# Attention's result in feature rows: division by sums broadcast over partitions, in place of two rounds of transposes

## The chip, the cores and the metric

One core of a Trainium2 chip. The metric is device time in microseconds of the whole kernel; the kernel before takes 807.38 us, the median of three runs (806.86 to 809.02). TensorE (PE in the profile) does the matmuls and the transposes, its weight loads are shown as PEld; VectorE is DVE, ScalarE is ACT, GpSimd is POOL, and SP issues DMAs.

## The reference

Attention over 2 x 8 heads of 768 positions with 64 features, in which a query sees only the keys of its own bucket (6 random hyperplanes hash both), and then two MLPs over 1536 tokens, 512 to 2048 to 512.

```python
mask = q_bucket[:, :, :, None] == k_bucket[:, :, None, :]
scores = np.where(mask, scale * np.matmul(q, k.transpose(0, 1, 3, 2)), -1000000000.0)
attn = np.exp(scores - np.max(scores, axis=-1, keepdims=True))
attn = attn / (np.sum(attn, axis=-1, keepdims=True) + 1e-09)
x = np.matmul(attn, v).transpose(0, 2, 1, 3).reshape(B * S, H * D)
x = softplus(x @ w_in) @ w_out                       # softplus: max(h, 0) + log1p(exp(-abs(h)))
h = x @ w2_in
return (h * np.clip(h + 3.0, 0.0, 6.0) / 6.0) @ w2_out
```

## The kernel before

The kernel writes no order of work by hand. Each step is added to a plan (`plan.add`) with the engines that may do it and a cost for each (A is ScalarE, D VectorE, P GpSimd, T TensorE, S an issue on SP), what it reads and writes, and a priority: the head's number times `TH` plus a constant of the table `WHEN`. For a DMA the plan also has a transfer time (`dma=`), and it lets a DMA go only when the eighth before it has landed. `Schedule.run` goes through modelled time, takes on each engine the ready step of lowest priority number, and emits it; the order of emission is the order on each engine's queue, and waits follow from buffers. Buffers with a tag and a number rotate: a new one waits until the last user of the old one is done.

Attention (`attend`, lines 413 to 529) runs per head over six tiles of 128 queries. Per tile: two halves of scores (lines 430 and 431, each a product of high parts and one of the rest and of the bucket bits), the negated row maximum on VectorE (444), a small step for bias and scale (451), exp on ScalarE (459) which also sums each row into `den`, six transposes of the result (470), and a copy out of PSUM into `et` (`even`, by the helper on lines 242 and 244). Scores and transposes share three PSUM buffers, `two0` to `two2`. When a head's six tiles are done, the values' product (486) runs in three steps. It gives `av`, 128 partitions by 384: partition u x 64 + d is feature d, column i x 128 + q is query q of tile 3u + i. So it comes with features in partitions, but two halves of the queries one above the other.

Behind it the kernel before goes to query rows and back. ScalarE copies `av` to `xa` (line 502), TensorE transposes its three blocks into PSUM (`pt`, line 508), GpSimd adds 1e-9 to the sums (512), VectorE takes the reciprocal (516) and multiplies, a reciprocal per partition and tile, into `xn` (523), queries in partitions, with 64 columns for each of two heads. When both heads of a pair are in, `to_features` (541 to 560) transposes the six tiles again (line 550, in groups of four and two) into `xt`, features of both heads in 128 partitions, and takes from PSUM the high part `xh` (ScalarE, line 242) and the rest `xl` (VectorE, line 247), the first MLP's input.

One PSUM bank each has the tags `pre` and `av`; the hash products `d` (372), `av`, `pt` and `xt` take whichever comes free, and later the first MLP's `ph`.

Beside attention the plan puts the loads of later heads and the weights of four of the MLPs' eight column blocks, each of which VectorE and ScalarE convert from two words to float pairs (lines 592 to 625). SP issues nearly all loads of the heads and the SBUF copies of query parts (359) and of bucket bits (403). The first MLP begins once the last scores are issued, between the last head's steps. The remaining weights are loaded when all buffers of the pool `tail` are done (`close_attention`).

Of the kernel before, what the change touches and what calls it, by code (L numbers as in the profile page):

```python
# [20 lines left out]
P = 128  # L21
# [10 lines left out]
BITS = 3  # L32
EX = 3

TH = 10.540
# [18 lines left out]
def f32(ap):  # L54
    return ap.bitcast(F32)
# [130 lines left out]
def lsh_attention_two_mlps(  # L186
# [33 lines left out]
    def open_pool(name, where, **kw):  # L220
        pools[name] = where.enter_context(tc.tile_pool(name=name, bufs=1, **kw))

    attention, heads = ctx.enter_context(ExitStack()), ctx.enter_context(ExitStack())
    for name in ("x", "w", "bits"):
        open_pool(name, ctx)
    open_pool("ps", ctx, space=PSUM)
    open_pool("tail", attention, side="right")
    open_pool("heads", heads)
# [11 lines left out]
    def cast(e, out, in_):  # L240
        if e == "A":
            nc.scalar.activation(out, in_, AF.Copy)  # L242
        else:
            engines[e].tensor_copy(out, in_)

    def minus(e, out, a, b):
        engines[e].tensor_tensor(out, a, b, op=ALU.subtract)
# [165 lines left out]
    def attend(h):  # L413
        at = h * TH
        if h % 2 == 0:
            xn[h // 2] = buffer("tail", [P, NT, P], F32, "xn", 2, f"xn{h // 2}")

# [74 lines left out]
        for c in range(0, NT, 2):  # L492
# [5 lines left out]
            ]  # L498
        xa = buffer("tail", [P, HALF], F32, "xa", 2, f"xa{h}")
        plan.add(  # L500
            dict(A=0.44), lambda e: cast(e, xa.ap, av.ap[:, :HALF]),
            reads=[av], writes=[xa], prio=at + WHEN["back"],
        )
        pt = buffer("ps", [P, 512], F32, ("pre", "av"), 1, f"pt{h}")

        def back(e):
            for i in range(n):
                nc.tensor.transpose(pt.ap[:, i * P : (i + 1) * P], xa.ap[:, i * P : (i + 1) * P], ident.ap)  # L508

        plan.add(dict(T=0.25), back, mode="t", reads=[xa, ident], writes=[pt], prio=at + WHEN["back"])  # L510
        plan.add(
# [6 lines left out]
        )  # L518
        x = xn[h // 2]

        def norm(e):
            place = x.ap.rearrange("p (u i) d -> p i u d", u=2)[:, :, :, (h % 2) * D : (h % 2 + 1) * D]
            nc.vector.tensor_tensor(
                place, pt.ap[:, :HALF].rearrange("p (i u d) -> p i u d", u=2, d=D),
                rec.ap.rearrange("p (u i) -> p i u", u=2).unsqueeze(3).to_broadcast([P, n, 2, D]), op=ALU.mult,
            )

        plan.add(dict(D=0.5), norm, reads=[pt, rec], writes=[x], prio=at + WHEN["norm"])
        return last_scores, exp

# [10 lines left out]
    def to_features(hp_all, first, n):  # L541
        b, hp = divmod(hp_all, H // 2)
        g, off = divmod(b * NT + first, 4)
        at = (2 * hp_all + 1) * TH
        pt = buffer("ps", [P, 512], F32, ("pre", "av"), 1, f"xt{hp_all}_{first}")
        place = lambda x: x[0, g].ap[:, hp, off * P : (off + n) * P]

        def turn(e):
            for i in range(n):
                nc.tensor.transpose(pt.ap[:, i * P : (i + 1) * P], xn[hp_all].ap[:, first + i, :], ident.ap)  # L550

        plan.add(dict(T=0.085 * n), turn, mode="t", reads=[xn[hp_all], ident], writes=[pt], prio=at + WHEN["x"])
        hi = plan.add(
            dict(A=0.053 + 0.107 * n), lambda e: cast(e, place(xh), pt.ap[:, : n * P]),
            reads=[pt], writes=[xh[0, g]], prio=at + WHEN["x_high"],
        )
        plan.add(
            dict(D=0.069 + 0.133 * n), lambda e: minus(e, place(xl), pt.ap[:, : n * P], f32(place(xh))),
            reads=[pt], writes=[xl[0, g]], prio=at + WHEN["x_low"], after=[hi],
        )  # L560
# [305 lines left out]
```

## Time and profile before

| | |
|---|---|
| median of three runs | 807.38 us |
| the profiled execution, its span | 806.4 us (1.0 us less than that median) |
| PE busy, matmuls and transposes | 780.0 us, 97% |
| PEld, weight loads | 598.0 us, 74% |
| VectorE busy | 533.9 us, 66% |
| ScalarE busy | 484.6 us, 60% |
| DMA moved | 58.6 MB, mean 73 GB/s |
| granted TensorE clock | full in all 40 slices |

The page gives the share of the whole span. Attention is the first third (to some 260 us), the MLPs the rest, and VectorE and ScalarE are far busier in the first than in the second. PE is busy in both, but its durations contain the way through the array and overlap, so what a matmul costs is read from the distance of two starts.

### The profile page before, as it was taken

Reading aid. Unit: us, or ns where it says so; the run is one execution under the profiler, and the core shown is the slowest. Engines: PE = TensorE matmul, PEld = TensorE weight load, DVE = VectorE, ACT = ScalarE, POOL = GpSimd, SP = SyncE. Lnnn points to the kernel's source line nnn. Section 1 sums busy time; section 2 is a strip of 40 time slices with the busy share of each in tenths; the row PEclk is TensorE's granted clock in tenths of the full one; section 3 lists DMA queues with packets and bytes.
Section 4 is the critical chain, followed back from the end, with each engine's and each line's share of the span. In section 5 each row is a group of like instructions: output and inputs, shape, how many; then the busy total and the mean of one; then the engine's idle time right before and its main releaser. Section 6 shows DMA issues by size and latency. Waiting matters only on the chain.

```text
span 806.4 us, 10352 instructions
## 1 busy us (share of the span) xinstructions
PE 780.0 (97%) x3808; PEld 598.0 (74%) x3808; DVE 533.9 (66%) x942; ACT 484.6 (60%) x817; POOL 9.4 (1%) x53
## 2 busy tenths in 40 slices
PE   6799999999999999999999999999999999999997
PEld 3466666666667777888888888878888888888886
DVE  6699899886765899965454799989952322232222
ACT  4688998888875877766555777766542322231222
POOL 1000000000000000000000000000000000000000
PEclk9999999999999999999999999999999999999999
DMA  6645445432310470000000355540000100010001
GB/s 176 163 138 143 125 149 149 124 111 73 89 30 15 154 260 2 0 1 1 0 1 1 104 207 185 183 156 1 1 0 1 53 0 1 1 52 1 1 0 53
DMA packets 26354, 58.61 MB, mean 73 GB/s; under 512 B 3584, under 2 KB 7552, under 8 KB 26304
## 3 DMA queue, kind: packets, MB, share of 16 engines
q1 hardware_dynamic: 22896, 49.56, 19.9%
q10 hardware_dynamic: 3408, 8.39, 3.2%
q8 instruction: 30, 0.49, 0.3%
q14 instruction: 20, 0.16, 0.1%
HBM read 48.89 MB, written 3.15 MB: 65 GB/s over the span
## 4 chain that ended last, share of the span: by engine, by line
PE 87%; ACT 7%; DVE 2%; DMA 2%; issue 1%; SPq 0%; ACTq 0%; DVEq 0%
PE ph L645 33%; PE acc L738 17%; PE acc L740 16%; PE av L486 7%; PE tp L470 6%; PE sc L430 4%; PE sc L431 3%; ACT e L459 3%; ACT et L242 2%; DMA raw<-in_moe_w_in_dram 1%; ACT qa L330 1%; DVE nm L444 1%; ACT ka L242 1%; PE pt L508 1%; PE xt L550 0%
## 5 line engine op out<-in xcount | busy, mean ns | idle before, releaser
L645 PE MATMUL ph<-xh,w 128*128 128x512 f32 x768 | 240.2, 394 | 0.0
L645 PEld LDWEIGHTS ph<-xh,w 128*128 128x128 f32 x768 | 143.9, 188 | 32.6
L645 PE MATMUL ph<-xl,w 128*128 128x512 f32 x384 | 151.1, 393 | 0.0
L674 DVE SCALAR_TENSOR_TENSOR ml<-me,ph 128x512 f32<-128x512 f32 x48 | 33.0, 688 | 117.8 <-ACT me L669 117.5
L669 ACT ACTIVATE me<-ph,three 128x512 f32<-128x512 f32 x48 | 33.1, 689 | 125.7 <-PE ph L645 122.8
L459 ACT ACTIVATE e<-sc,bs 128x768 f32<-128x768 f32 x96 | 94.8, 990 | 22.2 <-DVE bs L451 21.5
L444 DVE TENSOR_REDUCE nm<-sc 128x1 f32<-128x768 f32 x96 | 89.5, 951 | 25.6 <-PE sc L431 25.1
L738 PE MATMUL acc<-gh,w 128*128 128x512 f32 x384 | 98.9, 395 | 0.0
L740 PE MATMUL acc<-w,gh 128*128 128x512 f32 x384 | 98.0, 393 | 0.0
L470 PEld LDWEIGHTS tp<-ident,e 128*128 128x128 f32 x576 | 63.7, 142 | 37.1 <-ACT e L459 22.4
L470 PE MATMUL tp<-ident,e 128*128 128x128 f32 x576 | 80.0, 280 | 7.3 <-ACT e L459 6.2
L738 PEld LDWEIGHTS acc<-gh,w 128*128 128x128 f32 x384 | 71.3, 188 | 18.6 <-ACT gh L242 2.1
L645 PEld LDWEIGHTS ph<-xl,w 128*128 128x128 f32 x384 | 72.1, 188 | 16.8
L740 PEld LDWEIGHTS acc<-w,gh 128*128 128x128 f32 x384 | 72.1, 188 | 16.8
L430 PE MATMUL sc<-ka,qa 128*128 128x384 f32 x192 | 73.2, 381 | 6.4 <-ACT et L242 5.8
L486 PE MATMUL av<-et,vx 128*64 128x384 f32 x384 | 71.4, 497 | 0.0
L242 ACT ACTIVATE et<-tp 128x768 f32<-128x768 f32 x78 | 62.5, 811 | 12.6 <-PE tp L470 11.8
L431 PE MATMUL sc<-kb,qb 96*128 96x384 f32 x192 | 66.5, 346 | 0.4 <-DVE kb L384 0.4
L705 DVE SCALAR_TENSOR_TENSOR me<-mu,me 128x512 f32<-128x512 f32 x48 | 33.1, 690 | 36.6 <-ACT mu L700 36.6
L738 PE MATMUL acc<-gl,w 128*128 128x512 f32 x192 | 53.6, 393 | 0.7 <-ACT xh L242 0.7
L740 PE MATMUL acc<-w,gl 128*128 128x512 f32 x192 | 53.5, 393 | 0.0
L242 ACT ACTIVATE w<-bits 128x512 fp32r<-128x512 f32 x64 | 39.9, 628 | 21.1 <-DVE bits L616 21.1
(65 smaller groups left out, 948.2 us busy)
## 6 DMA issues: line engine op xcount, KB each, us to landing
raw<-in_moe_w_in_dram SPq DMA_DIRECT2D x24, 512.0 KB, 4.4
raw<-in_moe_w_out_dram SPq DMA_DIRECT2D x24, 512.0 KB, 3.5
rawk<-in_kv_dram SPq DMA_DIRECT2D x15, 384.0 KB, 3.6
raw<-in_moe_w_in_dram ACTq DMA_DIRECT2D x8, 512.0 KB, 4.1
raw<-in_moe_w_out_dram ACTq DMA_DIRECT2D x8, 512.0 KB, 3.8
raw<-in_kv_dram SPq DMA_DIRECT2D x16, 192.0 KB, 3.6
raw<-in_q_dram SPq DMA_DIRECT2D x16, 192.0 KB, 4.0
vx<-in_kv_dram SPq DMA_DIRECT2D x16, 192.0 KB, 2.5
```

Source lines behind the costliest of these rows:

```text
L242: nc.scalar.activation(out, in_, AF.Copy)
L430: nc.tensor.matmul(o, qa[h].ap[:, qs], ka[h].ap[:, cs], start=True, stop=False)
L431: nc.tensor.matmul(o, qb[h].ap[0:KB, qs], kb[h].ap[0:KB, cs], start=False, stop=True)
L444: lambda e, sc=sc, t=t: nc.vector.reduce_max(nm.ap[:, t, 0:1], sc.ap[:, :, :HALF], axis=AX.XY, negate=True),
L459: lambda e, sc=sc, ex=ex, t=t: nc.scalar.activation(ex.ap.rearrange("p (u k) -> p u k", u=2), sc.ap[:, :, :HALF], AF.Exp, bias=bs.ap[:, t, ...
L470: nc.tensor.transpose(o, ex.ap[:, c * P : (c + 1) * P], ident.ap)
L486: nc.tensor.matmul(av.ap[u * D : (u + 1) * D, :HALF], vx[h].ap[:, c, :], et[u].ap[:, c, :], start=(c == 0), stop=(c == NT - 1),)
L645: nc.tensor.matmul(bank(), w[:, a, :], x[b].ap[:, kc, :], start=(kc + i == 0), stop=(kc == KC - 1 and i == 2))
L669: dict(A=0.478), lambda e: nc.scalar.activation(e1.ap, bank(), AF.Relu, bias=three.ap),
L705: lambda e: nc.vector.scalar_tensor_tensor(e1.ap, u.ap, -1.0, e1.ap, op0=ALU.add, op1=ALU.subtract),
L738: nc.tensor.matmul(o, w.ap[:, a, cs], b.ap, start=st, stop=sp)
L740: nc.tensor.matmul(o, b.ap[:, cs], w.ap[:, a, :], start=st, stop=sp)
```

## The change

The result of the values' product stays with features in partitions. The reciprocals, which lie with queries in partitions, are written to DRAM (`row`), and from there read back twice with the partition broadcast over 64 partitions each into `wide`, whose columns are queries, with the three tiles side by side at every query (a step of three in the multiplication). VectorE multiplies `av` in PSUM by `wide` into `xa`. Two DMAs per head copy the halves of `xa` to `xn`, now 128 partitions of features by 768 queries, side by side. `to_features` takes `xh` and `xl` from `xn` in SBUF. The ScalarE copy of `av`, the three transposes `pt` per head and the six transposes `xt` per pair go. All five new DMAs are on SP; `wide` and `xa` have one buffer each. The constants in `WHEN` stay.

```diff
-            xn[h // 2] = buffer("tail", [P, NT, P], F32, "xn", 2, f"xn{h // 2}")
+            xn[h // 2] = buffer("tail", [P, S], F32, "xn", 2, f"xn{h // 2}")
...
-        xa = buffer("tail", [P, HALF], F32, "xa", 2, f"xa{h}")
-        plan.add(
-            dict(A=0.44), lambda e: cast(e, xa.ap, av.ap[:, :HALF]),
-            reads=[av], writes=[xa], prio=at + WHEN["back"],
-        )
-        pt = buffer("ps", [P, 512], F32, ("pre", "av"), 1, f"pt{h}")
-
-        def back(e):
-            for i in range(n):
-                nc.tensor.transpose(pt.ap[:, i * P : (i + 1) * P], xa.ap[:, i * P : (i + 1) * P], ident.ap)
-
-        plan.add(dict(T=0.25), back, mode="t", reads=[xa, ident], writes=[pt], prio=at + WHEN["back"])
...
-        def norm(e):
-            place = x.ap.rearrange("p (u i) d -> p i u d", u=2)[:, :, :, (h % 2) * D : (h % 2 + 1) * D]
-            nc.vector.tensor_tensor(
-                place, pt.ap[:, :HALF].rearrange("p (i u d) -> p i u d", u=2, d=D),
-                rec.ap.rearrange("p (u i) -> p i u", u=2).unsqueeze(3).to_broadcast([P, n, 2, D]), op=ALU.mult,
-            )
-
-        plan.add(dict(D=0.5), norm, reads=[pt, rec], writes=[x], prio=at + WHEN["norm"])
+        row = buffer("rows", [2, P, n], F32, "row", 2, f"row{h}")
+        wide = buffer("tail", [P, P, n], F32, "wide", WIDE, f"wide{h}")
+        xa = buffer("tail", [P, n, P], F32, "xa", 1, f"xa{h}")
+        plan.add(
+            dict(S=0.625),
+            lambda e: engines[e].dma_start(
+                out=row.ap.rearrange("u p i -> p u i"), in_=rec.ap.rearrange("p (u i) -> p u i", u=2)
+            ),
+            reads=[rec], writes=[row], prio=at + WHEN["rec"], dma=0.3,
+        )
+        for u in range(2):
+            plan.add(
+                dict(S=0.625),
+                lambda e, u=u: engines[e].dma_start(
+                    out=wide.ap[u * D : (u + 1) * D], in_=row.ap[u].partition_broadcast(D)
+                ),
+                reads=[row], writes=[wide], prio=at + WHEN["rec"], dma=0.55,
+            )
+        plan.add(
+            dict(D=0.5),
+            lambda e: nc.vector.tensor_tensor(
+                xa.ap, av.ap[:, :HALF].rearrange("p (i q) -> p i q", q=P), wide.ap.rearrange("p q i -> p i q"),
+                op=ALU.mult,
+            ),
+            reads=[av, wide], writes=[xa], prio=at + WHEN["norm"],
+        )
+        x, rows = xn[h // 2], slice(h % 2 * D, (h % 2 + 1) * D)
+        for u in range(2):
+            plan.add(
+                dict(S=0.625),
+                lambda e, u=u: engines[e].dma_start(
+                    out=x.ap[rows, u * HALF : (u + 1) * HALF], in_=xa.ap[u * D : (u + 1) * D].rearrange("p i q -> p (i q)")
+                ),
+                reads=[xa], writes=[x], prio=at + WHEN["back"], dma=0.35,
+            )
...
-        plan.add(dict(T=0.085 * n), turn, mode="t", reads=[xn[hp_all], ident], writes=[pt], prio=at + WHEN["x"])
         hi = plan.add(
-            dict(A=0.053 + 0.107 * n), lambda e: cast(e, place(xh), pt.ap[:, : n * P]),
-            reads=[pt], writes=[xh[0, g]], prio=at + WHEN["x_high"],
+            dict(A=0.053 + 0.107 * n), lambda e: cast(e, place(xh), x.ap[:, cols]),
+            reads=[x], writes=[xh[0, g]], prio=at + WHEN["x_high"],
         )
```

## Rows read from the trace of the kernel before

**Rows 1.** The page's chain that ended last: share of the span by engine.
```profile
PE 87%; ACT 7%; DVE 2%; DMA 2%; issue 1%; SPq 0%; ACTq 0%; DVEq 0%
```

**Rows 2.** Stretches: start:end, length, busy us (instructions) of PE, PEld, DVE, ACT, POOL.
```profile
48.00:176.00 128.00, 123.59 (x770) 83.61 (x770) 117.97 (x224) 113.15 (x198) 4.04 (x16) 1.00 0.48 138
176.00:256.00 80.00, 76.08 (x483) 52.41 (x480) 53.45 (x99) 62.67 (x110) 1.62 (x9) 1.00 0.20 53
256.00:806.00 550.00, 545.43 (x2387) 439.55 (x2385) 328.31 (x561) 278.92 (x465) 0.34 (x2) 1.00 0.15 52
```

**Rows 3.** Waits of PE, 48 to 256 us: in total, times, longest.
```profile
PE tp L470 <- ACT e L459: 3.6, 5, 1.1
PE sc L430 <- ACT et L242: 2.8, 6, 0.6
```

**Rows 4.** Groups, 0 to 300 us: count, busy us, mean ns, idle before.
```profile
L508 PE MATMUL pt<-ident,xa 128*128 128x128 f32 x48 | 7.9, 273 | 0.0
...
L550 PE MATMUL xt<-ident,xn 128*128 128x128 f32 x48 | 8.1, 283 | 0.7 <-DVE xn L523 0.7
...
L242 ACT ACTIVATE xa<-av 128x384 f32<-128x384 f32 x16 | 7.9, 492 | 1.6 <-PE av L486 1.4
...
L523 DVE TENSOR_TENSOR xn<-pt,rec 128x384 f32<-128x384 f32 x16 | 8.8, 550 | 0.1
...
L242 ACT ACTIVATE w<-bits 128x512 fp32r<-128x512 f32 x22 | 13.7, 629 | 1.2 <-DVE bits L616 1.2
...
L247 DVE TENSOR_TENSOR w<-bits,w 128x512 fp32r<-128x512 f32 x22 | 14.9, 682 | 0.9 <-ACT w L242 0.9
```

**Rows 5.** Timeline of PE around one pt group: start, length.
```profile
141.12 0.34 PE L430 MATMUL sc<-ka,qa 128*128 128x384 f32 x1
141.30 0.34 PE L431 MATMUL sc<-kb,qb 96*128 96x384 f32 x1
141.48 0.49 PE L508 MATMUL pt<-ident,xa 128*128 128x128 f32 x3
...
142.02 0.34 PE L431 MATMUL sc<-kb,qb 96*128 96x384 f32 x1
```

**Rows 6.** Timeline of PE around four xt transposes.
```profile
225.37 0.66 PE L550 MATMUL xt<-ident,xn 128*128 128x128 f32 x4
225.78 0.42 PE L430 MATMUL sc<-ka,qa 128*128 128x384 f32 x1
```

**Rows 7.** Tile xt: durations in ns, shortest, median, longest.
```profile
L242 ACT ACTIVATE xh<-xt x16: 382/490/617, 63.3 to 277.9; 128x512 fp32r<-128x512 f32 x8, 128x256 fp32r<-128x256 f32 x8
L247 DVE TENSOR_TENSOR xl<-xt,xh x16: 404/553/692, 64.4 to 278.5; 128x512 fp32r<-128x512 f32 x8, 128x256 fp32r<-128x256 f32 x8
```

**Rows 8.** The page's DMA issues: count, KB each, median us to landing.
```profile
qb<-bt SPq DMA_DIRECT2D x30, 48.0 KB, 1.9
...
qb<-qa SPq DMA_DIRECT2D x15, 192.0 KB, 2.7
...
p<-in_proj_dram ACTq DMA_DIRECT2D x1, 1.5 KB, 3.5
```

**Rows 9.** Timeline of VectorE: the reciprocals of heads 1 and 7.
```profile
50.09 0.18 DVE L516 RECIPROCAL rec<-rec 128x6 f32<-128x6 f32 x1
...
141.32 0.18 DVE L516 RECIPROCAL rec<-rec 128x6 f32<-128x6 f32 x1
```

**Rows 10.** Timeline of PE: the last values' product of heads 1 and 7.
```profile
54.72 1.51 PE L486 MATMUL av<-et,vx 128*64 128x384 f32 x8
...
149.20 1.51 PE L486 MATMUL av<-et,vx 128*64 128x384 f32 x8
```

**Rows 11.** Stretches, tile pt alone: PE, PEld, DVE busy us (instructions).
```profile
48.00:176.00 128.00, 3.94 (x24) 3.13 (x24) 4.41 (x9) 1.00 0.48 138
176.00:256.00 80.00, 2.46 (x15) 1.94 (x15) 3.01 (x6) 1.00 0.20 53
```

**Rows 12.** DMA issues from 27 to 29 us, same columns as rows 8.
```profile
qb<-qa SPq DMA_DIRECT2D x1, 192.0 KB, 5.7
```

More of the change, by code (lines that the diff above doesn't have):

```diff
@@ L33 @@
 EX = 3
+WIDE = 1
 TH = 10.540
@@ L226, in lsh_attention_two_mlps @@
     open_pool("ps", ctx, space=PSUM)
+    open_pool("rows", ctx, space=bass.MemoryType.DRAM)
     open_pool("tail", attention, side="right")
@@ L518, in attend @@
         )
-        x = xn[h // 2]
-        def norm(e):
-            place = x.ap.rearrange("p (u i) d -> p i u d", u=2)[:, :, :, (h % 2) * D : (h % 2 + 1) * D]
-            nc.vector.tensor_tensor(
-                place, pt.ap[:, :HALF].rearrange("p (i u d) -> p i u d", u=2, d=D),
-                rec.ap.rearrange("p (u i) -> p i u", u=2).unsqueeze(3).to_broadcast([P, n, 2, D]), op=ALU.mult,
-            )
-        plan.add(dict(D=0.5), norm, reads=[pt, rec], writes=[x], prio=at + WHEN["norm"])
+        row = buffer("rows", [2, P, n], F32, "row", 2, f"row{h}")
[15 more added lines that the diff above has]
+                reads=[row], writes=[wide], prio=at + WHEN["rec"], dma=0.55,
+            )
+        plan.add(
[15 more added lines that the diff above has]
+            )
         return last_scores, exp
@@ L544, in to_features @@
         at = (2 * hp_all + 1) * TH
-        pt = buffer("ps", [P, 512], F32, ("pre", "av"), 1, f"xt{hp_all}_{first}")
+        x = xn[hp_all]
+        cols = slice(first * P, (first + n) * P)
         place = lambda x: x[0, g].ap[:, hp, off * P : (off + n) * P]
-        def turn(e):
-            for i in range(n):
-                nc.tensor.transpose(pt.ap[:, i * P : (i + 1) * P], xn[hp_all].ap[:, first + i, :], ident.ap)
-        plan.add(dict(T=0.085 * n), turn, mode="t", reads=[xn[hp_all], ident], writes=[pt], prio=at + WHEN["x"])
         hi = plan.add(
-            dict(A=0.053 + 0.107 * n), lambda e: cast(e, place(xh), pt.ap[:, : n * P]),
-            reads=[pt], writes=[xh[0, g]], prio=at + WHEN["x_high"],
+            dict(A=0.053 + 0.107 * n), lambda e: cast(e, place(xh), x.ap[:, cols]),
+            reads=[x], writes=[xh[0, g]], prio=at + WHEN["x_high"],
         )
         plan.add(
-            dict(D=0.069 + 0.133 * n), lambda e: minus(e, place(xl), pt.ap[:, : n * P], f32(place(xh))),
-            reads=[pt], writes=[xl[0, g]], prio=at + WHEN["x_low"], after=[hi],
+            dict(D=0.069 + 0.133 * n), lambda e: minus(e, place(xl), x.ap[:, cols], f32(place(xh))),
+            reads=[x], writes=[xl[0, g]], prio=at + WHEN["x_low"], after=[hi],
         )
```

## The prediction

> **What bounds the kernel now.** I read the chain that ended last first: 87% of the span is on PE, and no DMA or other engine has more than 7% [rows 1]. The table by stretch comes next. From 256 us on PE is busy 545.4 of 550 us [rows 2]: the two MLPs run without a hole, so whatever attention gives back moves them forward whole. In attention PE is busy 123.6 of 128 us (48 to 176) and 76.1 of 80 us (176 to 256). The reader should compare these two: VectorE is busy 92% of the first (118.0 us) and 67% of the second (53.5 us), because the first also converts weights; yet PE issues 770 matmuls in 128 us and 483 in 80 us, 6.02 and 6.04 per us. Taking a quarter off VectorE's load changed nothing, so VectorE does not set the pace in either. The waits that stop the matmuls themselves, where the engine named is the true one, come to few: the two longest, behind exp and behind the copy of the transposed weights of attention, are 3.6 and 2.8 us in 208 us [rows 3]; the others are under 1 us each, and none is a DMA. Attention is bound by what PE has to issue, and the change takes from that.
>
> **What goes.** Per head three transposes (pt, line 508), per pair of heads six (xt, line 550): 48 and 48 in all [rows 4]. A busy PE is no price, since durations overlap, so I price them by starts. Two score matmuls in a row start 0.18 us apart (141.12 and 141.30); from the one at 141.30 the second next starts at 142.02 because three pt transposes lie between: 0.72 - 2 x 0.18 = 0.36 us for one pt group, the change of mode in and out included [rows 5]. Four xt take 225.37 to 225.78, 0.41 us, 0.10 each [rows 6]; where they stand alone they pay a mode change as pt does, 0.12 each. Per head that is 0.36 + 3 x 0.11 = about 0.70 us, over 16 heads 11.2 us. The bounds: at most the whole busy time of both groups, 7.9 + 8.1 = 16.0 us [rows 4]; at least nothing, if PE only waits longer where they were. ACT also loses xa, 16 x 0.49 = 7.9 us [rows 4], off an engine that has 113.2 of 128 us to do in the first stretch [rows 2]. Two of the four users of the PSUM banks "pre" and "av" go as well.
>
> **What stays the same size.** The multiplication by the reciprocal stays on VectorE with 128x384 results, one operand in PSUM: 0.55 us in the row [rows 4]. Its second operand now has a step of three elements in SBUF; no row shows such a step with two float tensors, so I bound it by nothing gained and by one full pass more (0.55 x 16 = 8.8 us on VectorE), and take zero: nearest to its own row. The casts xh and the remainders xl read SBUF where they read PSUM: at most 617 and 692 ns in the rows of before [rows 7], and 629 and 682 ns for the same 128x512 casts and subtractions from SBUF [rows 4]. Zero.
>
> **What is added.** Five DMAs per head, 80 in all, on SP: the reciprocals to DRAM (128 x 6 floats in runs of 12 bytes), two broadcast reads of 96 KB into wide, two SBUF copies of 96 KB into xn. None is shown. For the store I bound by the 48 KB copies, 1.9 us, and by the first load of proj, the row with the shortest runs, 3.5 us [rows 8]; I take 2.2, near the copies, which are issued in the same quiet queue. The broadcast lies between the 48 KB and the 192 KB SBUF copies, 1.9 and 2.7 us [rows 8]; I take 2.3, and 0.6 more for the issue of the second. Reciprocal to wide landed is then 2.2 + 0.6 + 2.3 = 5.1 us, with 4.4 and 6.8 as ends. It lies beside the values' product. In head 1 the reciprocal ends at 50.27 [rows 9] and the last matmuls of av at 56.23 [rows 10], 6.0 us; in head 7 at 141.50 and 150.71, 9.2 us. The shortest cover holds the middle estimate, and the normal one holds the upper end too. So the new wait of the multiplication costs nothing while av is what comes last. If the cover fails, VectorE stops at the multiplication, in order: behind it stand the row maxima of the next heads, behind these exp, and PE waits for exp to transpose. That is the rival below.
>
> On SP the store waits for the reciprocal and the broadcast for the store's landing, about 2 us with nothing else issued; behind them stand the loads of K, Q and V two heads ahead. Those land far ahead of use: none of PE's waits in 208 us is for a DMA [rows 3]. SP's work rises from nine to fourteen issues of about 0.6 us, 8.4 us of the 16 us that a head takes (24 pt matmuls, eight heads, in 128 us [rows 11]). Cost zero; if that slack were gone, up to 2 us per head. The copies into xn put about 3 us between the multiplication and the cast xh, where two transposes and a copy stood; xh is used only by the MLP, so nothing near it waits. At the end of attention PE has the first MLP's matmuls to issue meanwhile.
>
> **The sum.** Eight heads lie in 48 to 176, five in 176 to 256 [rows 11], two after and one before; that is the 39 and 9 of the 48 pt transposes. First stretch: 8 x 0.70 = 5.6 us off PE would bring VectorE to 118.0 of 122.4, 96%; two engines that full don't mesh, and I keep 70%, 3.9 us. Second: 3.5, of which 90%, 3.1 us, because VectorE and ACT (62.7 of 80 us) have room. The two after 256 stand between MLP matmuls without holes: 1.4 us. The first head lies in the start, where PE isn't full: zero. 3.9 + 3.1 + 1.4 = 8.4 us; 806.4 - 8.4 = 798.0 of span, and the median of the runs, 807.4, lies 1.0 above this span: 799.0 us. What isn't in the sum: the program that orders the work places all attention anew around the hole, by constants fitted to the old set of operations. I give it no sign, and 4 us to either side.
>
> **Rivals.**
> *VectorE sets the first stretch.* With 92% busy it is nearest to the limit there. If its order leaves it no more room, the first 3.9 us stay and only 3.1 + 1.4 = 4.5 us come: 802.9 us. For it: the 92%. Against: that the pace did not change when that load went. The Trainium skill speaks for it: "Perfetto Trace Analysis", "Identifying the Most-Contended Engine", has TensorE's headroom judged by the share of weight loads, not by matmul busy time, and the most occupied engine taken first; PEld is busy 83.6 of 128 us (65%) in that stretch against 92% on VectorE [rows 2], so by that rule taking PE work away there frees nothing. The even pace of 6.02 and 6.04 speaks against the rule.
>
> *The chain per query tile sets it.* Scores, maximum, exp, transposes and copy hand three PSUM buffers round; if that loop and not PE's issue sets the pace, what is removed turns into longer waits for exp and for the copy. Then only the part behind 256 us comes, 1.4 us: 806.0 us, no difference that can be told. For it: those are the very waits that exist [rows 3]. Against: they come to 6.4 us of 208.
>
> *The multiplication waits for wide, and it gets slower.* Beside weight loads, a 192 KB copy took 5.7 us to land against its median of 2.7 [rows 8, 12]. If the store and the broadcast each take 5.7 us, wide lands 5.7 + 0.6 + 5.7 = 12.0 us after the reciprocal, 2.8 us after the 9.2 us of cover. Over the ten heads or so (to some 170 us) beside which the first MLP's weights are loaded VectorE stops 28 us; with 8.4 us gained on PE it is 19.6 us slower, 827 us. It decides where reciprocal to wide exceeds some 9 us; at 7 us only a head with 6 us of cover notices. For it: that one landing, and that no row shows a store in 12-byte runs. Against: the median copies. The Trainium skill, "DMA: Bandwidth & Descriptors", "Queues, rings and completion order", says that a DMA's semaphore increment lands only after all earlier writes of that DMA engine, over all its queues; by that rule the small store is as late as the weights ahead of it, and the 5.7 us agrees, for the few microseconds in which weights move.
>
> **Chances.** The forecast, 794 to 802.5 us: 0.52. VectorE sets the first stretch, 802 to 805: 0.16. The chain sets it, within 0.3%, 2.4 us, of 807.4, about what a measurement of this kernel can tell from no change: 0.13. Slower by the wait for wide, or a part of it (three or four late heads, 811): 0.16. Better than forecast, because the freed banks let values and scores mesh and all 11.2 us or more come: 0.03. Faster is 0.52 + 0.16 + 0.03 = 0.71, the same 0.13, slower 0.16. The range goes from 791 (16.0 us off: 791.4) to 812, and leaves out most of the slow case and little else.
>
> **What would show it.** Right: pt and the transposes on xt gone; no other PE group grown; the first MLP matmul 7 to 10 us earlier; wide landed before av's last matmul in nearly all heads; VectorE above 94% in 48 to 170. Wrong: idle time of VectorE ahead of the multiplication that ends on a DMA; waits of the transposes for exp well above 3.6 us; the stretch from the first to the last score as long as before; or PE time in attention that falls less than 7 us with no wait to show for it, which would put it on the new order.

## The result, and the profile after

The changed kernel takes 817.1 us (median of four runs, 815.1 to 818.6) where the kernel before takes 807.2 beside it: 1.0113 times the time of before, 95% interval 1.0100 to 1.0126. (The ratio and its interval are those on record for the runs of both; the two medians alone give 1.012.) It is slower, and above the range, which ended at 812 us and so left out most of the slow case. The profiled execution has a span of 815.3 us against 806.4.

The first view is the page's chain that ended last; it answers to [rows 1].

```profile
PE 79%; DVE 8%; DMA 6%; ACT 4%; issue 2%; SPq 1%; DVEq 0%; ACTq 0%
```

DMA rose from 2% to 6% and VectorE from 2% to 8%: a chain that was nearly all TensorE now leaves it for VectorE and for DMAs. The table of stretches shows where, against [rows 2] (start:end, length, busy us and instructions of PE, PEld, DVE, ACT, POOL, then granted clock, DMA share, GB/s):

```profile
48.00:176.00 128.00, 112.89 (x645) 74.74 (x646) 111.91 (x209) 98.87 (x170) 3.33 (x14) 0.93 0.61 150
176.00:256.00 80.00, 76.42 (x467) 51.08 (x465) 60.82 (x109) 60.14 (x101) 2.10 (x10) 1.00 0.45 95
256.00:806.00 550.00, 548.45 (x2412) 441.13 (x2411) 329.74 (x567) 284.98 (x477) 0.57 (x3) 1.00 0.16 52
```

All of the loss is in the first stretch. PE idles 15.1 us there (4.4 before), the granted clock falls to 0.93, and VectorE does not go up to 96%, as forecast, but down to 87%. The starts of the heads' first scores say the same: from head 2 to head 8 they take 106.5 us (93.5 before), from head 10 to head 15 74.6 us (77.4 before). So the later heads do gain 0.56 us each, and the earlier ones lose 2.2 us each. The first MLP matmul starts at 271.6 us in place of 260.7.

The waits of PE, 48 to 256 us, answer to [rows 3] (total, times, longest):

```profile
PE tp L472 <- ACT e L461: 9.3, 8, 3.0
PE sc L432 <- ACT et L244: 5.8, 11, 1.2
```

Neither names a DMA (one lower row of the same view does, with 0.9 us for a load of V). One head shows how a late DMA turns into a wait for exp. Head 6, SP's queue first (start, length; an issue, not the transfer):

```profile
133.93 0.38 SPq L514 DMA_DIRECT2D row<-rec  x1
139.42 1.09 SPq L522 DMA_DIRECT2D wide<-row  x2
```

The reciprocal was ready at 133.90; the broadcast was issued 5.5 us after the store, as soon as that had landed. These are the landings in the same microseconds (median us from issue to landing):

```profile
wide<-row SPq DMA_DIRECT2D x2, 96.0 KB, 3.1
...
row<-rec SPq DMA_DIRECT2D x1, 3.0 KB, 5.5
```

VectorE around them (in brackets the idle time before an instruction):

```profile
138.43 0.69 DVE L626 SCALAR_TENSOR_TENSOR bits<-raw,bits 128x512 int32<-128x512 int32 x1
143.33 0.69 DVE L529 TENSOR_TENSOR xa<-av,wide 128x384 f32<-128x384 f32 x1 [4.21 <-PE sc L433]
143.92 0.69 DVE L249 TENSOR_TENSOR w<-bits,w 128x512 fp32r<-128x512 f32 x1
144.53 0.43 DVE L607 TENSOR_SCALAR bits<-bits 128x512 f32<-128x512 f32 x1
144.86 1.82 DVE L446 TENSOR_REDUCE nm<-sc 128x1 f32<-128x768 f32 x2
```

And PE:

```profile
138.07 1.53 PE L472 MATMUL tp<-ident,e 128*128 128x128 f32 x12
139.53 1.51 PE L488 MATMUL av<-et,vx 128*64 128x384 f32 x8
...
147.98 2.83 PE L472 MATMUL tp<-ident,e 128*128 128x128 f32 x12 [3.03 <-ACT e L461]
```

The reader should follow three steps. The values' product ends at 141.04, the second half of `wide` lands at 143.2, and the multiplication starts at 143.33 after 4.21 us of idle time: what it waited for is `wide`, although the row names PE. The scores that it names had just ended (143.26), but the multiplication does not read them; the product that it reads had been done for 2.2 us. Behind it stand two row maxima (144.86), behind these exp, and PE stops 3.03 us for exp. Then PE runs the same twelve transposes in 2.83 us that took 1.53 us ten microseconds earlier, at a granted clock of 0.50, which is 1.2 GHz: the clock falls at 146.6, 1.7 us into that stop, and is back at 153.5. The stretches show it as a mean (same columns as above):

```profile
128.00:144.00 16.00, 14.56 (x85) 10.67 (x85) 11.52 (x23) 12.66 (x23) 0.35 (x2) 0.89 0.60 160
144.00:160.00 16.00, 12.78 (x66) 9.41 (x65) 14.99 (x29) 10.44 (x18) 0.87 (x2) 0.79 0.49 99
160.00:176.00 16.00, 14.08 (x85) 9.02 (x84) 13.55 (x26) 13.34 (x23) 0.34 (x2) 1.00 0.72 163
```

The group of the multiplication answers to the one on L523 in [rows 4], the DMA issues from 44 to 176 us to [rows 8]:

```profile
L529 DVE TENSOR_TENSOR xa<-av,wide 128x384 f32<-128x384 f32 x16 | 10.8, 678 | 9.4 <-PE sc L433 5.7 <-PE sc L432 1.6 <-DMA wide<-row 1.1
```

```profile
raw<-in_moe_w_in_dram ACTq DMA_DIRECT2D x5, 512.0 KB, 6.0
...
wide<-row SPq DMA_DIRECT2D x16, 96.0 KB, 3.4
xn<-xa SPq DMA_DIRECT2D x15, 96.0 KB, 2.2
...
row<-rec SPq DMA_DIRECT2D x8, 3.0 KB, 5.0
```

From the reciprocal to the landing of `wide` it takes 8.3 to 13.3 us in heads 0 to 7 and 6.6 to 8.8 us in heads 8 to 15. In seven of the first eight heads `wide` is later than the end of the values' product, by 0.2 to 2.7 us, 12.2 us together; in the second eight it is never late: it lands 1.9 to 4.1 us before that end.

### The profile page after: what moved, and what is told of

Same layout as the page of the kernel before. It is cut to its first block, busy times and chain, and to the rows that moved or that the text cites. A ratio compares the mean times of both kernels' runs of the same rounds, so it can differ in the third digit from the quotient of the medians.

```text
span 815.3 us, 10300 instructions
## 1 busy us (share of the span) xinstructions
PE 776.0 (95%) x3712; PEld 591.3 (73%) x3712; DVE 539.7 (66%) x947; ACT 475.8 (58%) x796; POOL 9.4 (1%) x53
## 4 chain that ended last, share of the span: by engine, by line
PE 79%; DVE 8%; DMA 6%; ACT 4%; issue 2%; SPq 1%; DVEq 0%; ACTq 0%
PE ph L655 33%; PE acc L748 16%; PE acc L750 16%; PE av L488 5%; PE tp L472 5%; DVE nm L446 3%; PE sc L432 2%; PE sc L433 2%; DMA row<-rec 2%; ACT e L461 2%; DMA wide<-row 1%; ACT et L244 1%; DVE qa L339 1%; DMA raw<-in_moe_w_in_dram 1%; SPq L405 1%
## 5 line engine op out<-in xcount | busy, mean ns | idle before, releaser
L472 PEld LDWEIGHTS tp<-ident,e 128*128 128x128 f32 x576 | 66.8, 147 | 51.7 <-ACT e L461 32.4
L472 PE MATMUL tp<-ident,e 128*128 128x128 f32 x576 | 85.3, 291 | 16.2 <-ACT e L461 14.3
L244 ACT ACTIVATE et<-tp 128x768 f32<-128x768 f32 x73 | 58.1, 808 | 22.3 <-PE tp L472 22.1
L433 PE MATMUL sc<-kb,qb 96*128 96x384 f32 x192 | 66.4, 346 | 0.8 <-DVE kb L386 0.8
L432 PEld LDWEIGHTS sc<-ka,qa 128*128 128x128 f32 x192 | 37.7, 197 | 23.1 <-ACT et L244 15.1
```

Of the source, the lines that this page charges most:

```text
L432: nc.tensor.matmul(o, qa[h].ap[:, qs], ka[h].ap[:, cs], start=True, stop=False)
L433: nc.tensor.matmul(o, qb[h].ap[0:KB, qs], kb[h].ap[0:KB, cs], start=False, stop=True)
L472: nc.tensor.transpose(o, ex.ap[:, c * P : (c + 1) * P], ident.ap)
```

## Experiments

The theory after the result: the wait for `wide` costs most of the 10 us, the five DMAs cost something by themselves, and the transposes were worth less than forecast. Rivals were the new order of work, VectorE's load, SP's queue, and that the forecast's gain came whole and was lost again. Ratios are to the kernel before, run beside each kernel, with 95% intervals; us in the accounts are differences of these ratios times 807.3. Figures from a trace belong to the one execution of a kernel that was profiled.

### The wait, and the two DMAs behind it

**The multiplication reads a tile of ones** in place of `wide`. Order and DMAs are the same; the division is left out.

```diff
-                xa.ap, av.ap[:, :HALF].rearrange("p (i q) -> p i q", q=P), wide.ap.rearrange("p q i -> p i q"),
+                xa.ap, av.ap[:, :HALF].rearrange("p (i q) -> p i q", q=P), ones.ap.unsqueeze(1).to_broadcast([P, n, P]),
```

> The changed kernel with the order of every engine's queue kept, but the multiplication takes a constant tile of ones in place of wide: the division by the sums is left out. The store and the broadcast still run; nobody waits for them. Theory A (VectorE stands at the multiplication until wide has landed, exp and TensorE starve behind it and TensorE's clock falls): most of the loss goes, 796 to 801 us, idle time before the multiplication falls from 9.4 us to under 2, granted clock back to 1.0. Theory B (SP stands behind the store's landing and the five DMAs per head delay the loads and the weights): 810 us or more, since these stay. Theory C (the newly planned order is worse by itself): 813 to 817 us.

**As this, and the store and broadcasts aren't issued.**

> As the one before (ones in place of wide, same order), and the store and both broadcasts are not issued at all; only the copies into xn remain of the new DMAs. Theory A: within 2 us of the run before, 795 to 801. Theory B: 10 us or more below the run before. Theory C: 813 to 817 us.

Measured: 808.9 us, 1.0018 (1.0001 to 1.0035), and 806.1 us, 0.9985 (0.9969 to 1.0001). Both lie above what the theory expected, by 8 and 5 us from the ends of its ranges; it still counted the transposes at their full price. After against the first: the wait, with the dearer operand, costs 7.7 us. First against second: store and broadcasts that the multiplication doesn't wait for cost another 2.7 us. The traces, whose spans are 5.3 us apart, show where: the first kernel falls behind in two steps, at waits for other loads. One is 2.8 us, between the first scores of heads 1 and 2, where ScalarE waits 3.5 us for weights and in the second kernel 2.2. The other is 1.8 us, between those of heads 8 and 9, where ScalarE waits 1.9 us for weights and a hash product 0.6 us for Q; the second kernel has neither wait. And with store and broadcasts left out the change gains only 1.2 us, with an interval that includes none. The group of the multiplication in the kernel with ones:

```profile
L531 DVE TENSOR_TENSOR xa<-av,ones 128x384 f32<-128x384 f32 x16 | 8.8, 552 | 2.2 <-PE av L490 2.2
```

552 ns, as on L523 before (550); so 126 ns of the 678 are `wide` with its step of three, 2.0 us of VectorE over 16 heads. Its idle time falls from 9.4 to 2.2 us, and the granted clock from 48 to 176 us is 1.00 again:

```profile
48.00:176.00 128.00, 115.55 (x697) 74.62 (x697) 119.30 (x224) 105.06 (x181) 4.79 (x16) 1.00 0.65 155
```

**The 16 weight loads beside attention become memsets on GpSimd** (those weights are left out), all else as after.

> The changed kernel, same order, with the 16 weight loads that lie beside attention replaced by memsets on GpSimd (those weights are then wrong, the work on them stays). If the store and the broadcast are late because weights move on the same DMA engines: row lands in about 3.5 us as in the second half of attention, reciprocal to wide falls from 9 to 13 us to about 7 to 8 in every head, idle before the multiplication under 2 us, 798 to 803 us. If they are late behind the loads of K, Q on SP's own queue: row still 4 to 6 us in the first half and 808 us or more.

Measured: 807.0 us, 0.9990 (0.9976 to 1.0003). With the wait and all five DMAs in place the loss is gone. Reciprocal to `wide` is 6.3 to 9.1 us in heads 0 to 7, and only one head is late, by 1.1 us. The multiplication's group:

```profile
L529 DVE TENSOR_TENSOR xa<-av,wide 128x384 f32<-128x384 f32 x16 | 10.8, 675 | 2.4 <-PE av L488 1.8 <-DMA wide<-row 0.6
```

So the chain is late mainly because it runs beside the weight loads. Two limits go with that. Without these loads the store still has a median of 4.6 us and the chain takes 6.3 to 9.5 us over all heads. And this kernel is also spared what the loads cost otherwise, which was not measured on the kernel before: of 10 us less than after, 6.5 lie between the first scores of heads 2 and 8, but 3.0 ahead of head 2. A reader who takes the medians alone would miss it: the store's median over 44 to 176 us is 4.6 us here against 5.0. The worst ones decide: in after five of the first seven stores took 5.5 to 6.4 us, here none of these seven is over 4.7.

### Covers for the wait

Each of these computes all that after does. **The plan is told** that `row` and `wide` land 2 us later each.

```diff
-                op.done = free["M"] + DONE
+                op.done = free["M"] + DONE + op.lag
...
-            reads=[rec], writes=[row], prio=at + WHEN["rec"], dma=0.3,
+            reads=[rec], writes=[row], prio=at + WHEN["rec"], dma=0.3, lag=2.0,
```

> The changed kernel computing all of it; only the planner is told that the store and the broadcast land 2 us later each, so that it puts the multiplication, and the broadcast's issue on SP, later in the order. Theory A: VectorE has other work in that place, idle before the multiplication under 3 us, 797 to 804 us. Theory B: SP's work is the same, 810 us or more. Theory C: a new order, anything from 800 to 820.

**Store and broadcasts go to GpSimd's queue.**

```diff
-            lambda e: engines[e].dma_start(
+            lambda e: nc.gpsimd.dma_start(
```

> The changed kernel computing all of it, every compute engine's order kept; only the store and the two broadcasts are issued from GpSimd's queue and no longer from SP's. If the store is late because it lies behind loads of K and Q on SP's own queue, and SP's loads are late because SP stands behind the store: the reciprocal-to-wide time falls to 6 to 8 us also in the first half, idle before the multiplication under 3 us, 802 to 809 us. If it is the weight loads on the same DMA engines, the store stays at 4 to 6 us: 812 to 818 us.

**ScalarE copies `av` out, and the multiplication comes later,** in SBUF, per pair of heads.

> All of it computed in another way: ScalarE copies av out of PSUM as before the change, DMAs put the undivided halves into xn, and VectorE multiplies by wide once both heads of a pair are in, placed at least 4 us after the data by the planner; store and broadcasts on GpSimd's queue. Neither a PSUM bank nor VectorE's row maxima hang on the DMA chain. If the waits were the loss: 797 to 803 us, no idle time before the multiplication. If VectorE's load sets the first half: 803 to 808 us. If the new order is bad by itself: above 810.

**The order of before**, pt and xt not issued, with all changed operations put in their places: DMAs on GpSimd, two buffers for `wide`, and `xh` and `xl` one head later.

> All of it computed: the old order (planned with the transposes, which are then not issued), ScalarE's copy of av kept, the multiplication in the place of the old one, some 9 to 18 us behind the reciprocal, on SBUF; store, broadcasts and the copies into xn from GpSimd's queue, two buffers for wide; the casts xh and xl of a pair one head later. SP's order is that of before. If the wait for wide and the new order were the whole loss: 797 to 802 us, faster than both. If the five DMAs per head cost by themselves: 803 to 808 us. If the old place is still too early: idle time before the multiplication, 808 us or more.

Measured: 825.1 us, 1.0218 (1.0196 to 1.0239); 818.4, 1.0122 (1.0103 to 1.0141); 819.0, 1.0136 (1.0115 to 1.0157); 824.6, 1.0203 (1.0169 to 1.0237). None helps. With GpSimd's queue the store takes 2.7 to 7.6 us (2.5 to 6.4 on SP's) and the idle time before the multiplication is 12.1 us: it isn't SP's queue. In the other three this idle time is 0 to 1.1 us, so the wait is covered, and yet none is faster than the change. The PE waits of two of them, 20 to 290 us, the late plan first and then the old order, show the new places:

```profile
PE d L375 <- DMA raw<-in_q_dram: 10.2, 2, 6.0
PE tp L473 <- ACT e L462: 9.2, 12, 1.8
PE sc L433 <- ACT et L245: 8.3, 16, 1.6
```

```profile
PE sc L441 <- ACT et L244: 13.7, 14, 2.3
PE d L374 <- DMA raw<-in_q_dram: 7.2, 2, 3.8
PE tp L481 <- ACT e L470: 4.4, 5, 1.2
```

Now the hash products wait for the load of Q, which no matmul did before from 20 us on, and the waits for ScalarE's copy grow. In the old order ScalarE also stands 3.2 us until the copies into `xn` have read the one buffer of `xa`. And PE's clock falls as in after: from 40 to 290 us the granted clock stands at 0.50 for 13.7 to 20.5 us in these four kernels, against 17.1 in after and none before. So here an order that hid one wait exposed others; that this must be so isn't shown.

### The price of the DMAs alone

**Before, plus the five DMAs per head**, from GpSimd, read by nothing, all other work in the order of before; `xa`, which two of them read, has one buffer in place of two.

> The kernel before, complete, order kept on every queue; in addition GpSimd issues per head a store, two broadcasts and two copies of the same sizes as the change's, behind the reciprocal and behind the multiplication, and no engine reads what they bring. If five more DMAs per head cost by themselves, through later loads of K, Q and the weights: 813 to 822 us, the loads' median landing 0.5 us or more longer. If a DMA that nobody waits for costs nothing: 806 to 809 us.

Measured: 812.4 us, 1.0057 (1.0042 to 1.0071): 4.6 us for 80 DMAs that feed nothing, between the two expected ranges. The DMA issues from 44 to 176 us, in this kernel and then in the kernel before:

```profile
raw<-in_moe_w_in_dram ACTq DMA_DIRECT2D x6, 512.0 KB, 5.5
...
raw<-in_q_dram SPq DMA_DIRECT2D x9, 192.0 KB, 5.7
```

```profile
raw<-in_moe_w_in_dram ACTq DMA_DIRECT2D x6, 512.0 KB, 3.8
...
raw<-in_q_dram SPq DMA_DIRECT2D x9, 192.0 KB, 4.3
```

The loads beside them land 1.7 and 1.4 us later. Two waits, of those from 40 to 256 us, account for nearly all of the loss in this trace:

```profile
PE d L373 <- DMA raw<-in_q_dram: 2.0, 1, 2.0
...
ACT xa L243 <- PE sc L432: 2.9, 1, 2.9
```

The first, for Q, is the wait that the covers ran into as well; the kernel falls 1.7 us behind there, between heads 8 and 9. In the second the row names PE, but ScalarE's copy does not read those scores: it starts at 183.67, when the copies out of the one `xa` have landed (183.56), and the kernel falls another 2.2 us behind, between heads 10 and 11. So these DMAs feed nothing, and yet engines wait because of them. The 4.6 us are no price of DMAs by themselves: in this trace more than half of the loss goes with the missing second buffer.

### What the transposes were worth

**Before, without pt and xt**: their users read `xa` and `xn` in SBUF (so the result is left in the wrong rows); order of before.

> The kernel before with its order on every queue kept, and the transposes pt and xt not issued; the multiplication reads xa and the casts read xn in SBUF (so the rows are not turned: this part of the computation is left out). None of the new DMAs. Theory C (TensorE is the limit in the old order, and it is the new order that loses what the transposes give): 796 to 800 us, 7 to 11 us less than before, heads at 15.0 us or less. Theory D (the loop scores, maximum, exp, transposes, copy through three PSUM buffers sets the pace in the first half in any order): 803 to 807 us, the waits of TensorE for exp and for the copy longer by what the transposes took.

Measured: 804.4 us, 0.9967 (0.9954 to 0.9980): 2.7 us in place of 8.4. The waits of PE, 48 to 256 us:

```profile
PE sc L430 <- ACT et L242: 5.7, 9, 0.9
PE tp L470 <- ACT e L459: 4.2, 5, 1.2
```

9.9 us, against 6.4 in [rows 3]. One place shows the exchange. Before, then without the transposes, on PE (L470 transposes exp's result, L550 is xt):

```profile
125.18 0.88 PE L470 MATMUL tp<-ident,e 128*128 128x128 f32 x6
126.03 0.44 PE L550 MATMUL xt<-ident,xn 128*128 128x128 f32 x2
126.95 0.44 PE L430 MATMUL sc<-ka,qa 128*128 128x384 f32 x1 [0.49 <-ACT et L242]
```

```profile
122.71 0.87 PE L470 MATMUL tp<-ident,e 128*128 128x128 f32 x6
124.49 0.44 PE L430 MATMUL sc<-ka,qa 128*128 128x384 f32 x1 [0.91 <-ACT et L242]
```

From the transposes of exp's result to the next scores it is 1.77 us with the two xt between and 1.78 us without: the wait grew from 0.49 to 0.91 us, and xt was worth nothing here. ScalarE, before and then without the transposes, shows what the scores wait for:

```profile
123.35 0.81 ACT L242 ACTIVATE et<-tp 128x768 f32<-128x768 f32 x1
124.05 0.98 ACT L459 ACTIVATE e<-sc,bs 128x768 f32<-128x768 f32 x1
...
126.09 0.81 ACT L242 ACTIVATE et<-tp 128x768 f32<-128x768 f32 x1
```

```profile
120.89 0.79 ACT L242 ACTIVATE et<-tp 128x768 f32<-128x768 f32 x1
121.58 0.98 ACT L459 ACTIVATE e<-sc,bs 128x768 f32<-128x768 f32 x1
122.46 0.20 ACT L459 ACTIVATION_READ_ACCUMULATOR e<-sc,bs 128x1 f32 x1
122.55 0.62 ACT L242 ACTIVATE xh<-xn 128x512 fp32r<-128x512 f32 x1
123.07 0.66 ACT L592 ACTIVATE bits<-raw 128x512 f32<-128x512 f32 x1
123.64 0.80 ACT L242 ACTIVATE et<-tp 128x768 f32<-128x768 f32 x1
```

ScalarE is never idle here, but its two conversions, `xh` and `bits`, cost the scores nothing: the transposes of exp's result end at 123.58 (122.71 + 0.87), and the copy that frees the PSUM buffer starts 0.06 us later. What the scores wait for is the chain from exp through its transposes to the copy. From the start of exp to the scores it takes 2.91 us without xt and 2.90 with it, and xt was no part of it. Exp in its turn starts right behind the copy before it.

**The change without store and broadcasts, with 96 dummy transposes put back**, six behind each values' product.

> As e2_no_bounce (new order, ones in place of wide, no store, no broadcast), with six dummy transposes per head put back on TensorE behind the values' product, 96 in all, which nobody needs. If TensorE is the limit in the new order as well: 9 to 12 us over e2_no_bounce, 815 to 818. If TensorE has idle time in the first half of the new order and is full only in the second: 4 to 6 us over, 810 to 812. If it is nowhere the limit: within 3 us of 806.

Measured: 815.4 us, 1.0094 (1.0077 to 1.0111), 8.8 us over the same kernel without the dummies. In a place where nothing covers them 96 transposes cost 92 ns each, close to the 0.10 and 0.12 us of the forecast, though part of the 8.8 us is that the product now ends later (the multiplication idles 7.4 us for it).

### What holds attention, if not the issue of PE

**About half of VectorE's weight conversion left out** (two operations per weight tile, whose values are left out), in the change without store and broadcasts, and in the kernel before.

> As e2_no_bounce (ones in place of wide, no store, no broadcast), and of each weight conversion beside attention two of VectorE's steps are left out, 32 instructions of 0.68 us (these weights are then wrong); the order of the rest is kept. If VectorE sets the pace of heads 2 to 9 once nobody waits for wide: from 806 to 796 to 800 us, heads 3 to 9 at 15.2 us or less. If TensorE or the loop over three PSUM buffers sets it: 803 us or more.

> The kernel before with the same 32 steps of VectorE left out, the rest of the order kept. If VectorE was already the limit of the first half before the change: 800 to 804 us. If TensorE was, as predicted: 805.5 us or more, heads 3 to 9 still at 15.5 us.

**Some 23 us of ScalarE's casts moved to GpSimd**, in before, in before without the transposes, and there with VectorE relieved too.

> The kernel before, order kept on every queue, with two kinds of casts moved from ScalarE to GpSimd, which is idle: ka of the 15 later heads (0.85 us each) and the high part of the 16 weight blocks beside attention (0.63 us each), some 23 us of ScalarE in all. If ScalarE sets attention's pace: 798 to 803 us. If it is the loop over three PSUM buffers, or TensorE: 805.5 us or more; more than 808 if GpSimd is late with them.

> As e9_before_no_transposes (old order, pt and xt not issued), with the same casts on GpSimd: both TensorE and ScalarE are relieved. If the two are the limit together: 792 to 798 us. If the loop sets the pace: 802 to 805, as e9.

> As the one before, and VectorE's 32 steps of e7 left out as well: all three engines relieved, each by 11 to 23 us, in the old order. If any of them sets the pace: below 797 us. If the loop through PSUM with its fixed order sets it: 801 to 805 us.

**The row maximum over half of the columns**, which shortens a step of the loop from scores to copy; in before, and without the transposes.

```diff
-    nm.ap[:, t, 0:1], sc.ap[:, :, :HALF], axis=AX.XY, negate=True
+    nm.ap[:, t, 0:1], sc.ap[:, :, : HALF // 2], axis=AX.XY, negate=True
```

> The kernel before, order unchanged, with the row maximum of each half of the scores taken over the first half of its columns only (the output differs). That shortens one step of the loop scores, maximum, exp, transposes, copy by some 0.2 us per half, 0.4 us per tile; 96 tiles. If the latency of that loop through three PSUM buffers sets the pace of attention, 795 to 804 us. If the loop has slack and another limit (TensorE's issue, or the sum over an engine) sets the pace, 806 to 808 us, as the runs that relieved VectorE and ScalarE beside the loop gave.

> The same shorter maximum in the kernel before without its pt and xt transposes (their outputs are left unwritten). If the loop sets the pace, the time falls below both of its parts: under the short maximum alone by more than 3.2 us (what the transposes were worth with the long maximum), 789 to 800 us, since a shorter loop lets TensorE use what was taken off it. If the loop isn't the limit, 803 to 804.5 us, as without the transposes alone.

| kernel | us | ratio | interval |
|---|---|---|---|
| no store and broadcasts, less VectorE | 806.3 | 0.9978 | 0.9964 to 0.9992 |
| before, less VectorE | 807.7 | 0.9996 | 0.9984 to 1.0008 |
| before, less ScalarE | 807.4 | 0.9989 | 0.9980 to 0.9998 |
| no transposes, less ScalarE | 804.1 | 0.9948 | 0.9932 to 0.9963 |
| all three relieved | 803.8 | 0.9941 | 0.9924 to 0.9957 |
| before, short maximum | 806.6 | 0.9983 | 0.9974 to 0.9993 |
| no transposes, short maximum | 805.1 | 0.9970 | 0.9957 to 0.9983 |

With transposes, VectorE and ScalarE all relieved, the stretch from 48 to 176 us (columns as above) is this:

```profile
48.00:176.00 128.00, 120.67 (x721) 78.67 (x722) 105.13 (x197) 100.89 (x175) 17.96 (x37) 0.99 0.49 140
```

VectorE is down from 118.0 to 105.1 us, ScalarE from 113.2 to 100.9, PE from 123.6 to 120.7, and the kernel is 4.8 us faster than before. No engine's total set the pace. Nor does the maximum, in the kernel before: it takes 15 us off VectorE in that stretch, and the waits of PE stay as they were, 3.4 us for exp and 2.7 for the copy against 3.6 and 2.8.

## Why the prediction was wrong

**What bounds attention: the step that failed first.** The prediction took a PE that is busy 97% and waits 6.4 us of 208 as bound by what it issues. The order is fixed, and a wait stands where it stands: a transposed block ahead of a score matmul that waits for ScalarE's copy costs nothing, however busy PE looks. Of the 8.4 us 2.7 came. The unit prices were about right where nothing covers them (92 ns, as an upper end). The rival "the chain per query tile" said how it would go, longer waits for exp and for the copy, 806.0 us; without the transposes alone it is 804.4. Its cause is shown for a place, not for the whole: the scores at 124.49 wait for exp, its transposes and the copy, whose 2.9 us the removed transposes were no part of. Exp stands there behind a copy on ScalarE and not behind the maximum: the bias made from it was ready at 120.94, and in before at 123.41, both 0.6 us ahead of exp; that fits the shorter maximum, which brought 1.4 us. But moving casts away from ScalarE brings little too, so what it would take to shorten a head stays open. The other argument, that VectorE does not set the pace, held: less VectorE work brings nothing in before. The Trainium skill's rule that the prediction weighed ("Perfetto Trace Analysis", "Identifying the Most-Contended Engine") is right here that matmul busy time misleads (97% busy, and 96 transposes worth 2.7 us); its advice to take the most occupied engine first, VectorE, is not borne out (0.9996).

**Reciprocal to `wide`: sized wrong.** 2.2 + 0.6 + 2.3 = 5.1 us were taken, with 6.8 as the upper end; 8.3 to 13.3 us were measured in the first eight heads. The cover came out as taken from rows of before, 7.1 to 11.2 us in these heads; what failed is the time that it had to cover. The store, put near a 48 KB SBUF copy, has a median of 5.0 us and not 2.2 beside the weight loads, the broadcast 3.4 and not 2.3; even in the second half the store needs 3.6. The right row was there: the 5.7 us of a copy beside weight loads [rows 12]. It was set aside as one landing against a median of fifteen, though weights move beside half of the heads. The copies into `xn` took 2.2 us, which with the issue of the second is the 3 us that the prediction put there.

**The wait of the multiplication: the rival held.** Its mechanism was told right: VectorE stops at the multiplication, the maxima behind it, then exp, then PE. Its price was too high, since it made ten heads late by 2.8 us each; seven are late, by 12.2 us together, and 7.7 us are what the wait and the dearer operand cost at the end. The granted clock is a part of these 7.7 us that the prediction did not have. It stands at 0.50 for 17.1 us of that stretch (64.7 to 71.5, 129.6 to 133.0, 146.6 to 153.5), with ones in place of `wide` for none of it. Over all runs its mean is 0.986 in after and 0.994 with ones; in the ten runs without store and broadcasts the time goes from 803.6 us at 0.999 to 808.7 us at 0.988, some 0.5 us per 0.001. By that rate, as an estimate, up to 4 of the 7.7 us go with the lower clock that the stops bring; it is an upper end, since the rate contains the stops too. The Trainium skill, "DMA: Bandwidth & Descriptors", "Latency and other measured facts", gives about 2 us as the fixed cost of a DMA, and less under a lighter load of HBM. The quietest store here took 2.5 us and those beside the weights up to 6.4, so the trace agrees that load matters and lies above the figure.

**Five DMAs at nothing: wrong.** "None of PE's waits is for a DMA" showed that PE's loads had slack, not how much, and the weight loads had none for ScalarE. Its waits before, 5 to 260 us, have

```profile
ACT bits L592 <- DMA raw<-in_moe_w_in_dram: 4.5, 2, 3.8
```

The store and broadcasts cost 2.7 us without the multiplication waiting for them, through later loads of weights and Q. The 4.6 us of all five in the order of before are one such wait and one for the buffer `xa`.

**The operand with a step of three: taken as zero, it is 126 ns a head,** 2.0 us of VectorE in all. It was not tried by itself. Since 32 VectorE operations less brought 0.6 us in the change without store and broadcasts (0.9985 to 0.9978), it is not likely to be much of the 7.7.

**The new order, left without a sign: some 1.5 us slower,** from the kernel without transposes in the old order (0.9967) to the change without store and broadcasts (0.9985), in which the copies into `xn` are still issued; the two intervals overlap, so the sign is not certain. It lies within the 4 us that the prediction left to either side, but it is the net of two larger terms. Heads 4 to 7, by the starts of their scores, take 61.7 us before and 66.4 in the change without store and broadcasts, where nothing waits for `wide`; the seven heads from 8 on take 109.7 and 104.3. After takes 71.2 us for heads 4 to 7, so half of its loss there comes without the wait. VectorE's load is not the reason (67.9 us with less of it), nor are the weight loads (68.3 without them); what it is stays open.

The account from 807.3: -2.7 for the transposes, +1.5 for order and copies, +2.7 for store and broadcasts, +7.7 for the wait and the operand make +9.2, the 1.0113 that was measured. The terms are differences along a row of neighbouring kernels, so they add up by construction, which confirms none of them; each is uncertain by one to two microseconds. What is open is what the new order costs in heads 4 to 7, and what bounds a head of some 15.5 us.

No kernel with the whole division by DMA came under the time of before. The short maximum is 0.2% faster than before, but it rests on the maximum of half a row being near enough to that of the whole, so it is no candidate.

## What to carry to other kernels

Before you price removed work on a busy engine, look at what stands right behind each piece in that engine's order: where it is a wait for another engine, the piece can have been free. A result that takes two dependent DMAs needs a cover that holds under the traffic of its own stretch: take the slowest landing beside that traffic, not the median of a quiet one. Where a DMA reads a buffer that is written again soon, count the wait for that too. And an engine that a row names as the releaser is to be checked against what the waiting instruction reads from it; here the DMA that was to blame hardly shows in the list of waits.

## What the runs showed of the hardware

A store of 3 KB in runs of 12 bytes took 2.5 and 2.6 us in the quiet heads 14 and 13 and up to 6.4 us beside weight loads; SP waited 50.2 us in all for the 16 of them:

```profile
SPq L522 <- DMA row<-rec: 50.2, 16, 5.9
```

From another engine's queue it was no faster (up to 7.6 us). After a stop of 3.03 us PE ran twelve transposes in 2.83 us in place of 1.53, at a granted clock of 0.50 (1.2 GHz) that held until 153.5 us: this stop cost more than its own length.
